# One crossbar transpose a chunk for q and k together, issued one or two loads behind the chunk's own load

## The chip, the cores and the metric

The kernel runs on one core of a Trainium2 chip. The metric is the device time of one execution in microseconds (us), median of several runs; the profile shows one execution, whose span is 1.7 to 1.9 us shorter than its time. Engines: PE is TensorE, POOL is GpSimd, DVE is VectorE, ACT is ScalarE, SP is the sequencer that issues nearly all DMAs here, in program order. The "rings" of the text are the queues that hold issued transfers for the DMA engines; a transfer "lands" when its data has arrived.

## The reference

Retention (8 batches, 8 heads, 576 tokens of 64), then a gated feed-forward block over 4608 tokens:

```python
scores = scale * np.matmul(q, k.transpose(0, 1, 3, 2))
Dmat = np.where(rel >= 0, gamma[:, None, None] ** rel[None, :, :], 0.0)
attn = np.matmul(scores * Dmat, v)                     # (B, H, S, D)
x = attn.transpose(0, 2, 1, 3).reshape(B * S, H * D)   # 4608 x 512
gate = 1.0 / (1.0 + np.exp(-(x @ w_gate)))             # d_ff = 1536
out = (gate * (x @ w_val)) @ w_out
```

## The kernel before

Tokens are cut into 40 chunks, five a batch: four of 128 tokens and one of 64. Chunks 0 to 3 go another way; chunks 4 to 39 are the subject. For each, three loads (v, k, q; 256 KB each) bring fp32 tiles; POOL scales and casts k into a block-diagonal tile, scales and casts q, and casts v; SP transposes k and q through the crossbar; PE makes scores (`qk`), updates a running state (`st`, copied to SBUF by DVE as `sbd`) and combines both (`pv`). The feed-forward matmuls of finished tokens fill PE between these phases.

```python
def cast_k(s):
    ...
    kn = kbd[s % 3]                      # block-diagonal, wiped once
    for j in range(n // 64):
        for hh in range(2):
            nc.gpsimd.tensor_tensor(out=kn[half(hh), j, :, half(hh)], in0=k32[half(j), hh::2, :], ...)

def cross(s):
    ...
    t = att_pool.tile([P, 2, M, P], BF16, tag="kT", bufs=3)     # 8 blocks of 128 columns
    nc.sync.dma_start_transpose(out=t[:, 0:nj]..., in_=natural["k", s][:, 0:nj]...)
    t = att_pool.tile([P, M, P], BF16, tag="qT", bufs=5)        # 4 blocks
    nc.sync.dma_start_transpose(out=t[:, :, 0:n], in_=natural["q", s][0:n]...)

def casts_to(s):
    while done["cast"] <= min(NS - 1, s):
        x = done["cast"]
        cast_k(x); cast_q(x); cross(x); cast_v(x)
        done["cast"] += 1

def run_phase(kind, s):
    if kind == "qk":
        loads_to(s + LEAD_LOAD)          # 5
        casts_to(s + LEAD_CAST)          # 2
        phase_qk(s)
        ...
```

So at the scores of chunk s, SP is given the loads up to s + 5 and then the transposes of s + 2: three chunks' loads stand ahead of a transpose.

Of the kernel before, what the change touches and what calls it, by code (L numbers as in the profile page):

```python
# [10 lines left out]
BF16 = mybir.dt.bfloat16  # L11
# [5 lines left out]
def kernel(  # L17
# [19 lines left out]
    nc = tc.nc  # L37

    B, H, S, D = q.shape
    NT, DM = out.shape  # L40
    DFF = moe_w_gate.shape[1]
    P = 128
    M = H // 2
# [4 lines left out]
    consts = ctx.enter_context(tc.tile_pool(name="consts", bufs=1))  # L48
    ld_pool = ctx.enter_context(tc.tile_pool(name="ld", bufs=18))
    nat_pool = ctx.enter_context(tc.tile_pool(name="nat", bufs=4))  # L50
    att_pool = ctx.enter_context(tc.tile_pool(name="att", bufs=3))
# [13 lines left out]
    STEPS = [(b, c) for b in range(B) for c in range(NC)]  # L65
    width = [min(P, S - c * P) for c in range(NC)]
# [8 lines left out]
    def load(s):  # L75
        b, c = STEPS[s]
        n = width[c]
        t0 = c * P
        tiles = []
        for nm, src in (("v", v), ("k", k), ("q", q)):  # L80
            t = ld_pool.tile([P, H, D], FP32, tag="ld", name=f"{nm}32_{s}")
            nc.sync.dma_start(out=t[0:n], in_=src[b, :, t0:t0 + n, :].rearrange("h p d -> p h d"))
            tiles.append(t)
        loaded[s] = tiles
# [21 lines left out]
    def load_wo(f):  # L106
        t = ld_pool.tile([P, DM], FP32, tag="ld", name=f"wo32_{f}")
        nc.sync.dma_start(out=t, in_=moe_w_out[f * P:(f + 1) * P, :])
        parts["o", f] = t
# [6 lines left out]
    load(4)  # L116
    load_w(8, 4)
    load(5)
    for f in range(3):
        load_wo(f)  # L120
    LEAD_LOAD = 5
    LEAD_CAST = 2


# [3 lines left out]
    def fill(n):  # L128

        ps = ffn_psum.tile([P, 512], FP32, tag="ffn", name=f"idle_{fill.at}")  # L130
        fill.at += 1
        for i in range(n):
            nc.tensor.matmul(ps, lhsT=blank[:, 0:P], rhs=blank, start=True, stop=True)
# [37 lines left out]
                                base=0, pattern=[[-1, 2], [1, P]], channel_multiplier=-2)  # L171
    NB = 4
    vbd = [consts.tile([P, 2, M, P], BF16, name=f"vbd{i}") for i in range(NB)]
    kbd = [consts.tile([P, 2, M, P], BF16, name=f"kbd{i}") for i in range(3)]
    tri = consts.tile([P, 64], BF16)

    def later_constants():

        nc.gpsimd.memset(tri, 1.0)
        for p0 in (0, 64):  # L180
            nc.gpsimd.affine_select(out=tri[p0:p0 + 64], in_=tri[p0:p0 + 64], compare_op=ALU.is_ge, fill=0.0,
                                    base=0, pattern=[[1, 64]], channel_multiplier=-1)
        for t in kbd:
            nc.gpsimd.memset(t, 0.0)


# [4 lines left out]
    def cast_w(nm, f, nf, i, eng):  # L191
        r = NKC // nf
        at = (slice(None), slice(i * r, (i + 1) * r), slice(f * P, (f + nf) * P))
        eng(out=(wg_sb if nm == "g" else wv_sb)[at], in_=parts.pop((nm, f, i)))  # L194
# [9 lines left out]
    natural = {}  # L204
    turned = {}
# [13 lines left out]
    def cast_k(s):  # L219

        b, c = STEPS[s]
        n = width[c]
        k32 = loaded[s][1]
        kn = kbd[s % 3]
        for j in range(n // 64):
            for hh in range(2):
                nc.gpsimd.tensor_tensor(  # L227
                    out=kn[half(hh), j, :, half(hh)], in0=k32[half(j), hh::2, :],
                    in1=ktab[half(j), c, hh::2].unsqueeze(2).to_broadcast([64, M, D]), op=ALU.mult)
        natural["k", s] = kn  # L230

    def cast_q(s):
        b, c = STEPS[s]
        n = width[c]
        q32 = loaded[s][2]
        qs = nat_pool.tile([P, H, D], BF16, tag="qs", name=f"qs_{s}")
        nc.gpsimd.tensor_tensor(out=qs[0:n], in0=q32[0:n],  # L237
                                in1=qtab[0:n, c, :].unsqueeze(2).to_broadcast([n, H, D]), op=ALU.mult)
        natural["q", s] = qs

    def cast_v(s):

        b, c = STEPS[s]
        n = width[c]
        v32 = loaded[s][0]
        vb = vbd[s % NB]
        for j in range(n // 64):
            for hh in range(2):
                nc.gpsimd.tensor_copy(out=vb[half(hh), j, :, half(hh)], in_=v32[half(j), hh::2, :])  # L249
        natural["vb", s] = vb  # L250

    def cast_dense(s, j):

        if s >= NS or STEPS[s][1] == NC - 1:
            return
        if j == 0:
            natural["vs", s] = nat_pool.tile([P, 2, M, D], BF16, tag="vs", name=f"vs_{s}", bufs=2)
        for hh in range(2):
            nc.scalar.copy(out=natural["vs", s][half(hh), j], in_=loaded[s][0][half(j), hh::2, :])  # L259

    def cross(s):

        n = width[STEPS[s][1]]
        nj = n // 64
        t = att_pool.tile([P, 2, M, P], BF16, tag="kT", name=f"kT_{s}", bufs=3)
        nc.sync.dma_start_transpose(out=t[:, 0:nj].rearrange("p j m t -> p (j m) t"),
                                    in_=natural["k", s][:, 0:nj].rearrange("p j m d -> p (j m d)"))
        turned["k", s] = t
        t = att_pool.tile([P, M, P], BF16, tag="qT", name=f"qT_{s}", bufs=5)
        nc.sync.dma_start_transpose(out=t[:, :, 0:n],  # L270
                                    in_=natural["q", s][0:n].rearrange("p h d -> p (h d)"))
        turned["q", s] = t

    turned = {}

# [5 lines left out]
    def half(x):  # L281
        return slice(x * 64, x * 64 + 64)
# [46 lines left out]
    def tile_sv(s, eng):  # L329
        sb = sbd[s % 4]  # L330
        for hh in range(2):
            eng(out=sb[half(hh), :, half(hh)], in_=st_tiles[STEPS[s][0]][half(hh)])
        state[s, 1] = sb
# [28 lines left out]
    def phase_qk(s):  # L362
        n = width[STEPS[s][1]]
        nj = n // 64
        kT, qT = turned["k", s], turned["q", s]
        pt = att_pool.tile([P, M, P], BF16, tag="pt", name=f"pt_{s}")
        qkp = qk_psum.tile([P, M, P], FP32, tag="qk", name=f"qk_{s}")
        for j in range(nj):
            for m in range(M):
                nc.tensor.matmul(qkp[:, m, half(j)], lhsT=kT[:, j, m, :], rhs=qT[:, m, half(j)],  # L370
                                 start=True, stop=True)
        nc.vector.tensor_tensor(out=pt[:, :, 0:n].rearrange("p m (j t) -> p m j t", t=64),  # L372
                                in0=qkp[:, :, 0:n].rearrange("p m (j t) -> p m j t", t=64),
                                in1=tri.unsqueeze(1).unsqueeze(1).to_broadcast([P, M, nj, 64]), op=ALU.mult)
        probs[s] = pt

    def phase_pv(s):
        b, c = STEPS[s]
        n = width[c]
        t0 = first_tok[s]  # L380
        qT = turned["q", s]
        pt = probs.pop(s)
        vb = natural["vb", s]
        pvp = pv_psum.tile([P, M, P], FP32, tag="pv", name=f"pv_{s}")
        for j in range(n // 64):
            before = state.get((s, j - 1) if j else (s - 1, 1)) if c or j else None
            for m in range(M):
                if before is not None:
                    nc.tensor.matmul(pvp[:, m, half(j)], lhsT=before[:, m, :], rhs=qT[:, m, half(j)],  # L389
                                     start=True, stop=False)  # L390
                nc.tensor.matmul(pvp[:, m, half(j)], lhsT=vb[:, j, m, :], rhs=pt[:, m, half(j)],  # L391
                                 start=before is None, stop=True)
        nc.scalar.copy(out=xT[:, :, t0:t0 + n], in_=pvp[:, :, 0:n])  # L393
# [27 lines left out]
    done = {"ld": PAIRED + 2, "cast": PAIRED}  # L421

    def loads_to(s):
        while done["ld"] <= min(NS - 1, s):
            load(done["ld"])
            done["ld"] += 1

    def casts_to(s):
        while done["cast"] <= min(NS - 1, s):
            x = done["cast"]  # L430
            cast_k(x)
            cast_q(x)
            cross(x)
            cast_v(x)
            done["cast"] += 1

    def run_phase(kind, s):
        if kind == "qk":
            loads_to(s + LEAD_LOAD)
            casts_to(s + LEAD_CAST)  # L440
            phase_qk(s)
            cast_dense(s, 1)
        elif kind == "pv":
            phase_pv(s)
            cast_dense(s + 1, 0)
        else:
            phase_st(s, int(kind[2]))
# [146 lines left out]
    cast_pair("k", 1, 0, nc.gpsimd)  # L594
    cast_pair("k", 1, 1, nc.gpsimd)
    tile_sv(1, on_act)
    fill(3)

    h_first((0,), 0, 2 * P)
# [34 lines left out]
    casts_to(4)  # L634
    for i in range(4):
        cast_w("g", 8, 4, i, on_pool)
    for f in range(3, 8):
        load_wo(f)
    casts_to(5)
    for f in range(8, NFC):  # L640
        load_wo(f)
    loads_to(6)
# [19 lines left out]
        cast_wo(f, on_pool)  # L662
    loads_to(7)
    casts_to(6)
    loads_to(8)
    h_first((10, 11), 0, 4 * P)
    at = 0

# [62 lines left out]
```

## Time and profile before

| | before |
|---|---|
| time, median of 3 | 359.12 us (359.04 to 359.7) |
| span of the profiled run | 357.5 us |
| PE idle, 57.7 to 103.7 us | 13.3 us |
| PE waits for a transposed q | 12.0 us, 6 times |
| POOL waits for PE's states (buffer of k) | 66.7 us, 30 times |
| transposes | 72 |

The page's first part gives busy times, its second 40 equal slices of the span. Lists by engine name a line of the kernel, what it writes and reads, and what ended the idle time before it. The lines that carry the reading stand in the prediction below.

### The profile page before, as it was taken

What the parts mean: (1) busy time and instruction counts of PE and PEld (TensorE: products, weight loads), DVE (VectorE), ACT (ScalarE), POOL (GpSimd) and SP (SyncE); (2) the same over time, 40 slices, a digit from 0 to 9 for tenths busy, and PEclk for the clock granted to TensorE, in tenths of its full rate; (3) what the DMA queues carried; (4) which work ended last, traced back from release to release, by engine and by line L of the source; (5) the groups of instructions that cost most, each with busy time, mean ns of one, the idle gap of its engine ahead of it and who ended that gap; (6) DMA issues with size and microseconds to landing.
All of it is one profiled execution on the core that took longest, in us unless ns stands there. A gap on an engine that the chain in (4) does not pass through costs nothing.

```text
span 357.5 us, 7682 instructions
## 1 busy us (share of the span) xinstructions
PE 334.3 (94%) x2868; PEld 191.7 (54%) x2868; DVE 162.9 (46%) x344; ACT 171.2 (48%) x356; POOL 187.5 (52%) x335
## 2 busy tenths in 40 slices
PE   7899985967699999999999899999999999999996
PEld 3565443855575655655655555554455545544443
DVE  4656520534374653742644653553356345512420
ACT  6765324424455645545545555544465455533321
POOL 7446657958682796367534894576437950000000
PEclk9999999889999999999999999999999999999999
DMA  8999999999999999996997999997599440011002
GB/s 227 314 329 286 251 265 173 208 217 215 181 178 210 212 138 211 212 181 139 166 163 164 161 172 242 211 156 155 148 175 204 115 113 14 0 61 59 2 25 93
DMA packets 169396, 60.27 MB, mean 169 GB/s; under 512 B 152848, under 2 KB 161296, under 8 KB 169360
## 3 DMA queue, kind: packets, MB, share of 16 engines
q1 hardware_dynamic: 169216, 59.66, 84.0%
q8 instruction: 22, 0.36, 0.4%
q14 instruction: 14, 0.11, 0.2%
q10 hardware_dynamic: 144, 0.13, 0.1%
HBM read 37.75 MB, written 9.44 MB: 132 GB/s over the span
## 4 chain that ended last, share of the span: by engine, by line
PE 73%; DMA 10%; POOL 9%; issue 3%; DVE 1%; ACT 1%; SPq 1%; POOLq 0%; DVEq 0%; ACTq 0%
PE h L464 43%; PE op L527 20%; POOL kbd L227 5%; DMA qT<-qs 3%; POOL vbd L249 2%; PE qk L370 2%; PE st L403 2%; POOL qs L237 2%; DMA kT<-kbd 2%; DMA k<-in_k_dram 2%; PE pv L391 2%; DMA q32p<-in_q_dram 1%; PE pv L389 1%; DMA v<-in_v_dram 1%; DMA wo<-in_moe_w_out_dram 1%
## 5 line engine op out<-in xcount | busy, mean ns | idle before, releaser
L227 POOL TENSOR_TENSOR kbd<-k,ktab 64x256 bf16<-64x256 f32 x128 | 78.5, 613 | 86.5 <-PE st L403 66.7
L464 PE MATMUL h<-xT,wv_sb 128*128 128x512 bf16 (+3 forms) x592 | 119.5, 325 | 0.2 <-ACT g L487 0.2
L464 PE MATMUL h<-xT,wg_sb 128*128 128x512 bf16 (+3 forms) x592 | 119.3, 325 | 0.0
L491 DVE TENSOR_TENSOR gv<-g,h 128x512 bf16<-128x512 bf16 (+1 forms) x104 | 65.2, 627 | 69.0 <-PE h L464 53.1
L487 ACT ACTIVATE g<-h 128x512 bf16<-128x512 f32 (+1 forms) x104 | 56.9, 548 | 70.8 <-PE h L464 60.9
L527 PE MATMUL op<-wo_sb,gv 128*128 128x512 bf16 x372 | 85.5, 379 | 0.0
L464 PEld LDWEIGHTS <-wg_sb 128*128 128x128 bf16 x592 | 53.0, 100 | 35.3 <-issue 0.3
L464 PEld LDWEIGHTS <-wv_sb 128*128 128x128 bf16 x592 | 53.1, 100 | 32.9 <-DVE wv_sb L194 0.6
L409 DVE CAST sbd<-st 64x256 bf16<-64x256 f32 x112 | 47.1, 421 | 16.3 <-PE st L403 13.9
L372 DVE TENSOR_TENSOR pt<-qk,tri 128x512 bf16<-128x512 f32 (+1 forms) x36 | 22.7, 630 | 68.8 <-PE qk L370 68.5
L527 PEld LDWEIGHTS <-gv 128*128 128x128 bf16 x372 | 34.4, 98 | 36.3
L249 POOL CAST vbd<-v 64x256 bf16<-64x256 f32 x128 | 50.8, 397 | 4.9
L259 ACT CAST vs<-v 64x256 bf16<-64x256 f32 x112 | 45.1, 403 | 1.8
L499 ACT COPY ob<-op 128x512 f32<-128x512 f32 x35 | 20.3, 587 | 53.1 <-PE op L527 42.9
L237 POOL TENSOR_TENSOR qs<-q,qtab 128x512 bf16<-128x512 f32 (+1 forms) x36 | 37.6, 1044 | 2.8
L393 ACT CAST xT<-pv 128x512 bf16<-128x512 f32 (+1 forms) x36 | 19.4, 538 | 27.5 <-PE pv L391 27.4
L370 PE MATMUL qk<-qT,kT 128*128 128x64 bf16 x256 | 13.7, 196 | 12.0 <-DMA qT<-qs 12.0
L370 PEld LDWEIGHTS <-kT 128*128 128x128 bf16 x256 | 12.7, 99 | 18.5 <-DMA kT<-kbd 10.8
L477 ACT ACTIVATE g<-h 128x256 bf16<-128x256 f32 x32 | 12.2, 384 | 20.2 <-PE h L464 18.4
L403 PEld LDWEIGHTS <-kbd 128*128 128x128 bf16 x224 | 13.6, 98 | 15.3 <-POOL kbd L227 3.3
L403 PE MATMUL st<-vs,kbd 128*128 128x64 bf16 x224 | 15.8, 193 | 3.6 <-DVE sbd L409 3.0
L391 PE MATMUL pv<-pt,vbd 128*128 128x64 bf16 x256 | 19.2, 193 | 0.0
(66 smaller groups left out, 178.8 us busy)
## 6 DMA issues: line engine op xcount, KB each, us to landing
out_dram<-ob SPq DMA_DIRECT2D x35, 256.0 KB, 2.3
v<-in_v_dram SPq DMA_DIRECT2D x28, 256.0 KB, 3.9
k<-in_k_dram SPq DMA_DIRECT2D x28, 256.0 KB, 4.4
q<-in_q_dram SPq DMA_DIRECT2D x28, 256.0 KB, 5.0
wg<-in_moe_w_gate_dram SPq DMA_DIRECT2D x12, 256.0 KB, 5.7
wv<-in_moe_w_val_dram SPq DMA_DIRECT2D x12, 256.0 KB, 5.6
wo<-in_moe_w_out_dram SPq DMA_DIRECT2D x12, 256.0 KB, 3.9
k32p<-in_k_dram SPq DMA_DIRECT2D x4, 256.0 KB, 4.7
```

The lines of the kernel that those rows point to most:

```text
L227: nc.gpsimd.tensor_tensor(out=kn[half(hh), j, :, half(hh)], in0=k32[half(j), hh::2, :], in1=ktab[half(j), c, hh::2].unsqueeze(2).to_broadc ...
L237: nc.gpsimd.tensor_tensor(out=qs[0:n], in0=q32[0:n], in1=qtab[0:n, c, :].unsqueeze(2).to_broadcast([n, H, D]), op=ALU.mult)
L249: nc.gpsimd.tensor_copy(out=vb[half(hh), j, :, half(hh)], in_=v32[half(j), hh::2, :])
L259: nc.scalar.copy(out=natural["vs", s][half(hh), j], in_=loaded[s][0][half(j), hh::2, :])
L370: nc.tensor.matmul(qkp[:, m, half(j)], lhsT=kT[:, j, m, :], rhs=qT[:, m, half(j)], start=True, stop=True)
L391: nc.tensor.matmul(pvp[:, m, half(j)], lhsT=vb[:, j, m, :], rhs=pt[:, m, half(j)], start=before is None, stop=True)
L403: nc.tensor.matmul(st_tiles[b][:, m, :], lhsT=natural["k", s][:, j, m, :], rhs=natural["vs", s][:, j, m, :], start=(c == 0 and j == 0 and ...
L409: nc.vector.tensor_copy(out=sb[half(hh), :, half(hh)], in_=st_tiles[b][half(hh)])
L464: nc.tensor.matmul(out, lhsT=w_sb[:, kc, fc * P:(fc + 1) * P], rhs=xT[:, kc, t0 + a:t0 + e], start=(kc == 0), stop=(kc == NKC - 1))
L487: nc.scalar.activation(out=g[:, 0:n], in_=h1[:, 0:n], func=AF.Sigmoid)
L491: nc.vector.tensor_tensor(out=gvs[some[0]][:, a:e], in0=g[:, 0:n], in1=h2[:, 0:n], op=ALU.mult)
L527: nc.tensor.matmul(opp, lhsT=gvs[fc][:, nb * P:(nb + 1) * P], rhs=wo_sb[:, fc, :], start=(fc == 0), stop=(fc == NFC - 1))
```

## The change

Its intent: halve the transposes by laying q and the two diagonal k blocks side by side in one tile, and bring each transpose out from behind the loads of later chunks. The natural tile has four buffers, not three; two are wiped by DVE early on. The core of the diff:

```diff
-    for f in range(3):
+    for f in range(2):
         load_wo(f)
-    kbd = [consts.tile([P, 2, M, P], BF16, name=f"kbd{i}") for i in range(3)]
+    qk_nat = [consts.tile([P, 3, M, P], BF16, name=f"qk_nat{i}") for i in range(NB)]   # NB = 4
@@ cast_k, cast_q
-        kn = kbd[s % 3]
+        kn = qk_nat[s % NB][:, 1:3]
-        qs = nat_pool.tile([P, H, D], BF16, tag="qs", name=f"qs_{s}")
+        qs = qk_nat[s % NB][:, 0].rearrange("p m (hh d) -> p (m hh) d", d=D)
@@ cross: the two transposes give way to
+        nb = 1 + width[STEPS[s][1]] // 64
+        t = att_pool.tile([P, 3, M, P], BF16, tag="T", name=f"T_{s}", bufs=4)
+        nc.sync.dma_start_transpose(out=t[:, 0:nb].rearrange("p j m t -> p (j m) t"),
+                                    in_=qk_nat[s % NB][:, 0:nb].rearrange("p j m d -> p (j m d)"))
@@ casts_to, run_phase
             x = done["cast"]
+            loads_to(x + (1 if x < 10 else 2))
             cast_k(x)
...
-            loads_to(s + LEAD_LOAD)
             casts_to(s + LEAD_CAST)
```

In the start-up part chunk 5's casts are written out, so that they pull no loads forward, and the early load of chunk 8 goes.

## The prediction

> **What bounds the kernel now.** I read the page first, for busy time and its 40 slices. TensorE (PE) is the bound almost everywhere:
>
> ```profile
> PE 334.3 (94%) x2868; PEld 191.7 (54%) x2868; DVE 162.9 (46%) x344; ACT 171.2 (48%) x356; POOL 187.5 (52%) x335
> ...
> PE   7899985967699999999999899999999999999996
> ...
> PEclk9999999889999999999999999999999999999999
> ```
>
> The span is 357.5 us and PE is busy 334.3, so 23.2 us is all that can be won by feeding PE sooner, plus what two dips of its clock cost. The slices that are not full stand at both ends and from the seventh to the twelfth, about 54 to 107 us. Busy time by stretch puts a number on it:
>
> ```profile
> 0.00:45.00 45.00, 41.59 (x411) 23.07 (x412) 25.46 (x63) 25.91 (x52) 26.16 (x50) 1.00 1.04 281
> 45.00:57.70 12.70, 11.40 (x90) 5.68 (x88) 2.81 (x6) 5.12 (x12) 7.34 (x13) 1.00 1.18 252
> 57.70:103.70 46.00, 32.67 (x435) 27.82 (x435) 18.48 (x54) 18.49 (x46) 34.63 (x62) 0.93 1.05 190
> 103.70:190.00 86.30, 86.12 (x734) 51.23 (x733) 42.72 (x87) 44.80 (x97) 50.06 (x90) 1.00 1.03 182
> 190.00:220.00 30.00, 28.24 (x270) 16.65 (x268) 15.97 (x33) 16.78 (x37) 23.09 (x41) 1.00 1.23 179
> ```
>
> First is the stretch and its length, then PE's busy time. Between 57.7 and 103.7 us PE idles 46.00 - 32.67 = 13.3 us; between 190 and 220, 1.8 us; from 103.7 to 190 only 0.2. So the question is what PE waits for in the third row. The table of waits:
>
> ```profile
> PE qk L370 <- DMA qT<-qs: 12.0, 6, 4.2
> ...
> PE st L403 <- DVE sbd L409: 3.0, 5, 1.0
> ```
>
> 12.0 us in six waits is the arrival of a transposed q: chunk 6 at 61.96 us (4.23 us of waiting), chunk 7 at 75.17 (2.34), chunk 8 at 83.03 (1.43), chunk 9 at 91.24 (0.37), chunk 10 at 97.14 (2.77): 11.1 us in this stretch. The sixth, 0.9 us, falls after 200 us. Why it is late stands in the timeline of the DMA-issuing queue (start, length, issue):
>
> ```profile
> 57.42 1.87 SPq L266 DMA_TRANSPOSE kT<-kbd  x1
> 59.38 1.21 SPq L270 DMA_TRANSPOSE qT<-qs  x1
> ...
> 65.26 0.57 SPq L82 DMA_DIRECT2D v<-in_v_dram  x1
> 65.87 1.11 SPq L82 DMA_DIRECT2D k<-in_k_dram  x1
> 67.03 1.46 SPq L82 DMA_DIRECT2D q<-in_q_dram  x1
> 68.59 3.86 SPq L266 DMA_TRANSPOSE kT<-kbd  x1
> 72.55 1.20 SPq L270 DMA_TRANSPOSE qT<-qs  x1
> ```
>
> Chunk 7's casts end on GpSimd (POOL) at 64.05 us, but its transposes stand behind the loads of chunks 8, 9 and 10: k goes out at 68.59, that issue takes 3.86 us because the rings are full, q follows at 72.55 and lands 2.6 us later. Thus **PE waits for an order in a queue**, not for DMA or POOL capacity; both are busy but neither is full (POOL works 34.63 of 46 us).
>
> **The Trainium skill.** (1) "DMA: Bandwidth & Descriptors", section Queues, rings and completion order: descriptors are consumed in ring order on each DMA engine. The 3.86 us issue behind nine loads agrees. (2) The same page, section Rules for kernel authors: coalesce many small transfers. The trace agrees only in part: with nothing else moving (274 to 293 us) a four-block transpose issues in 1.20 us and an eight-block one in 1.23 to 1.31, so issue time is nearly free of size; but the landing grows from 2.4 to about 3.4 us for 512 more packets of 256 B. (3) "TensorE: Matmul & The Clock Gate", section The HAM clock gate: after an idle window of about 3.4 us the clock halves. The trace agrees: 0.51 granted from 61.4 to 64.8 us, 0.50 from 75.1 to 78.5, just after the two longest idle stretches of this part. No page tells what twelve blocks cost; my figure is worked out from the trace.
>
> **The change, part by part.**
>
> *One transpose for two.* A full chunk is now one transfer of twelve blocks, not eight and four; the bytes stay (a half-width chunk moves eight blocks, not six). Issue: 36 issues of about 1.2 us go. Latency in a quiet queue: before, k issue 1.3 plus q's 2.6 to land is about 4.0 us; after, 3.4 plus 1.0 for 512 more packets is an estimated 4.4 us. So merging alone gains nothing for one chunk, and q's early half no longer starts before q is cast (k used to go out one cast, 1.04 us, earlier). Its gain is the issue time where the queue is the limit: from 37 to 52 us SP issues without pause, and chunks 4 and 5 save 1.24 and 1.47 us there, so the load of chunk 6 goes out about 2.5 us sooner than the 49.1 us of before.
>
> *Transposes ahead of loads.* For chunk x only the load of x+1 (x under 10) or x+2 stands ahead, where three more chunks stood. A chunk's load is 3072 packets of 256 B; the trace moves about 855 of them in a microsecond, 3.6 us a chunk. A transpose takes about 2.4 us of the engines.
>
> *Four buffers, not three,* for the natural k: POOL waited 66.7 us in 30 times for PE to finish the states of three chunks back. It may now run a chunk (some 5.6 us of POOL) further ahead.
>
> *Wipes.* POOL wipes two tiles of 1536 columns for three of 1024, the same work. Two more wipes go to DVE near 14 us; 512 columns of the same kind took 0.48 us, so 768 take an estimated 0.72 each, 1.44 in all, in a gap of 1.63 us (13.87 to 15.50). Nothing on the path.
>
> *The new schedule worked out* (my arithmetic, from the durations above and 5.54 us of POOL a chunk, the distance from chunk 7's first cast at 60.29 us to chunk 8's at 65.83):
> - k of chunk 6 lands near 52.4 us (54.7 before), its casts end near 56.3, the transpose lands near 60, after load 7 leaves the engines. PE needs it at 56.8. Start of chunk 6 on PE: 60, against 61.96: **2 us won.** If the load does not come sooner, it lands at 62.8 and 0.9 us is lost here.
> - Chunk 7 lands near 66, chunk 8 near 72, chunk 9 near 79. PE's own work puts its needs at 60 + 10.6 = 70.6, then 75.5, then 83.3: no wait. I took PE's distances between chunks from the trace and left out the DMA waits; the second clock dip (3.4 us at half, about 1.5 us lost) goes with the wait before it.
> - Chunk 10 waits for two loads ahead of it (11 and 12, where the lead changes from one to two, and a store that follows PE): an estimated 88.7, needed at 86.7. A **new wait of 2 us.** Chunk 11 lands about 95.5, needed at 95.0.
> - So chunk 11 starts on PE near 95.5, where the trace has 103.3 to 103.5: **8 us won.** Chunk 12 was needed only at 112.06, so from there PE is full again.
> - 190 to 215 us: POOL runs chunk after chunk at about 6 us and PE idles 1.8 us for it. One more chunk of lead covers this: **1.3 us**, less than the whole as the DMA share is at its highest there.
>
> Sum: 8 + 1.3 = 9.3 us, 359.1 - 9.3 = 349.8, taken as **350 us**. The stages before 45 us and after 220 are the same work and PE is full in both.
>
> **The rivals.**
>
> *POOL or the load takes over the wait.* With one load of lead, POOL may finish a chunk and find the next k not landed: 3.6 us of load behind 2.4 of transpose and up to three stores (256 KB at some 340 GB/s, 0.75 us each) is over 7 us against POOL's 5.5. For: the queue is in order, so every wait for POOL also holds back the next load. Against: I have counted most of this and slack of 3 to 4 us is left at chunks 7 to 9. If it bites at each chunk by 1 us more, half the gain goes: about 354 to 355 us.
>
> *The merged transfer is slow.* Between two transposes in a row the engines moved only 97 to 99 GB/s (59 to 60, 72 to 74 us) though they count as busy; twelve blocks could be as slow all through. Then chunk 6 starts later than before and the whole string shifts by 2 to 3 us: about 353. The opposite, that the gap between the two transfers is what is slow and goes, would give 347.
>
> *The waits were hidden anyway.* The wait of PE for DVE's states (3.0 us) and the DMA rate stay. Against: the six waits fall on PE, the bound, and the idle time of the stretch matches them. If only the order mattered for chunk 7 and others fell back on POOL, 355 to 356.
>
> *A loss* would need transposes in the full stretch after 104 us to come late with the shorter lead. PE uses a chunk each 8.9 us there ((316 - 103) / 24), POOL and DMA need an estimated 5.5 to 6.9, so I give it little.
>
> **Range and chances.** The middle is 350. If the load of chunk 6 comes no sooner I get about 352.5 to 353, with that and the first rival 355; with both clock dips gone and no new wait at chunk 10, 346.5. Faster by over 2% means below 351.9, and my middle is only 2 us under it: 0.64. Within 2%: 0.34. Slower: 0.02.
>
> **What the changed profile should show.** PE busy in about 57 to 96 us of 80% or more, not 71%. The total of PE's waits for transposes down from 12.0 to 4 to 6 us, the longest still at chunk 6 (about 3 us), one at chunk 10. The SP timeline with one transpose of 1.3 to 2 us issue a chunk, landing in 4 to 5.5 us. The clock dip at 75 us gone. POOL's waits for PE's states well below 66.7 us before 110 us, with some waits for k loads in their place. Idle time near 190 to 215 below 1 us. I am wrong if chunk 6 starts later than 62 us, if POOL's waits for k loads grow past 5 us between 60 and 100, or if PE shows new gaps after 110 us.

## The result, and the profile after

The changed kernel took **353.8 us** (352.06 to 354.28, 4 runs) beside 359.41 us (359.04 to 359.9, 4 runs). The ratio is 0.9839, 95% interval 0.9806 to 0.9872. Ratios here are the mean time of one kernel's fast runs over the mean of the other's fast runs of the same rounds, so not quite the ratio of the medians. The time lies in the predicted range, 3.8 us above the predicted middle, and the change falls within 2%, the outcome to which the prediction gave a chance of 0.34. The profiled run was the fastest (352.06 us), so I ran the kernel again (below: 353.26 us); where the two profiles differ I say so.

The page after, same parts as the prediction's first fence:

```profile
PE 332.4 (95%) x2868; PEld 190.5 (54%) x2868; DVE 163.7 (47%) x346; ACT 171.2 (49%) x356; POOL 187.7 (54%) x334
...
PE   7899994987999999999999999999999999999996
...
PEclk9999998799999999999999999999999999999999
```

PE's work is the same 2868 matmuls; the weak slices now end four slices sooner. Busy time by stretch (stretch and its length, then PE's busy time; the last three numbers are the granted clock, the DMA share and GB/s):

```profile
57.70:103.70 46.00, 38.83 (x493) 31.40 (x494) 22.08 (x62) 21.19 (x51) 36.97 (x67) 0.93 1.10 212
59.50:66.30 6.80, 5.41 (x57) 5.41 (x58) 2.42 (x7) 1.04 (x3) 6.21 (x11) 0.50 1.13 230
75.10:78.50 3.40, 3.10 (x70) 3.08 (x71) 1.44 (x6) 1.80 (x5) 0.45 (x1) 1.00 1.32 237
190.00:220.00 30.00, 28.93 (x258) 16.06 (x257) 16.61 (x34) 15.79 (x34) 23.25 (x42) 1.00 1.24 210
```

The idle time between 57.7 and 103.7 us fell from 13.3 to 7.2 us, that between 190 and 220 from 1.8 to 1.1. The half-rate clock at 75 us is gone, but 6.8 us of it now stand in one piece after the wait at chunk 6, as much as the two dips of before together; the repeat has 3.4 us (0.51 from 62.4 to 65.8). What PE still waits for:

```profile
PE qk L365 <- DMA T<-qk_nat: 5.1, 2, 4.5
PE st L398 <- DVE sbd L404: 4.6, 7, 1.9
```

12.0 us of waits for transposes became 5.1, nearly all at chunk 6; PE's waits for DVE's states grew from 3.0 to 4.6 us (in the repeat 2.4 us are put down to DVE and 2.2 to POOL). That PE now comes to them sooner is my reading. The queue of DMA issues, against the 68.59 and 72.55 us of before for chunk 7:

```profile
62.60 1.42 SPq L264 DMA_TRANSPOSE T<-qk_nat  x1
64.12 1.94 SPq L501 DMA_DIRECT2D out_dram<-ob  x3
66.11 0.66 SPq L82 DMA_DIRECT2D v<-in_v_dram  x1
66.82 0.70 SPq L82 DMA_DIRECT2D k<-in_k_dram  x1
67.56 0.63 SPq L82 DMA_DIRECT2D q<-in_q_dram  x1
68.31 2.94 SPq L264 DMA_TRANSPOSE T<-qk_nat  x1
```

Chunk 7's transpose goes out at 62.60 us, when its casts end, and chunk 8's follows in 5.7 us with three stores and one load (the 64 tokens of chunk 9) between. On POOL the wait changed its name, first the kernel before, then the changed one:

```profile
POOL kbd L227 <- PE st L403: 66.7, 30, 7.5
POOL kbd L227 <- DMA k<-in_k_dram: 9.9, 3, 5.5
```

```profile
POOL qk_nat L227 <- DMA k<-in_k_dram: 31.3, 11, 9.5
...
POOL qk_nat L227 <- PE st L398: 7.6, 6, 1.8
```

With the shorter lead POOL waits for loads, not for buffers. Between 60 and 100 us that is 4.8 us of it, in two waits; later it costs little, as PE idles 0.3 us from 103.7 to 190.

### The profile page after: what moved, and what is told of

It is laid out like the page before. It is cut to its first block, busy times and chain, and to the rows that moved or that the text cites. A ratio compares the mean times of both kernels' runs of the same rounds, so it can differ in the third digit from the quotient of the medians.

```text
span 350.2 us, 7624 instructions
## 1 busy us (share of the span) xinstructions
PE 332.4 (95%) x2868; PEld 190.5 (54%) x2868; DVE 163.7 (47%) x346; ACT 171.2 (49%) x356; POOL 187.7 (54%) x334
## 4 chain that ended last, share of the span: by engine, by line
PE 75%; DMA 9%; POOL 5%; DVE 3%; issue 3%; SPq 3%; ACT 2%; POOLq 0%; DVEq 0%; ACTq 0%
PE h L459 42%; PE op L522 22%; DMA k<-in_k_dram 5%; DMA T<-qk_nat 3%; POOL qk_nat L227 3%; PE qk L365 2%; PE st L398 2%; PE pv L386 2%; PE pv L384 2%; DMA q32p<-in_q_dram 1%; DVE sbd L404 1%; POOL qk_nat L237 1%; POOL vbd L248 1%; SPq L82 1%; PE op L512 1%
## 5 line engine op out<-in xcount | busy, mean ns | idle before, releaser
L227 POOL TENSOR_TENSOR qk_nat<-k,ktab 64x256 bf16<-64x256 f32 x128 | 78.4, 613 | 69.2 <-DMA k<-in_k_dram 31.3
L459 PEld LDWEIGHTS <-wg_sb 128*128 128x128 bf16 x592 | 53.0, 100 | 35.4 <-issue 0.3
L404 DVE CAST sbd<-st 64x256 bf16<-64x256 f32 x112 | 47.0, 420 | 15.7 <-PE st L398 13.3
L367 DVE TENSOR_TENSOR pt<-qk,tri 128x512 bf16<-128x512 f32 (+1 forms) x36 | 22.7, 630 | 62.8 <-PE qk L365 62.5
L237 POOL TENSOR_TENSOR qk_nat<-q,qtab 128x512 bf16<-128x512 f32 (+1 forms) x36 | 37.5, 1042 | 3.1 <-DMA q<-in_q_dram 0.4
L398 PEld LDWEIGHTS <-qk_nat 128*128 128x128 bf16 x224 | 13.6, 98 | 16.3 <-POOL qk_nat L227 3.5
L398 PE MATMUL st<-vs,qk_nat 128*128 128x64 bf16 x224 | 15.8, 194 | 4.8 <-DVE sbd L404 4.6
L365 PEld LDWEIGHTS <-T 128*128 128x128 bf16 x256 | 12.2, 99 | 11.4 <-DMA T<-qk_nat 5.9
L365 PE MATMUL qk<-T 128*128 128x64 bf16 x256 | 13.6, 195 | 5.1 <-DMA T<-qk_nat 5.1
```

The costliest lines, as they stand in the source:

```text
L237: nc.gpsimd.tensor_tensor(out=qs[0:n], in0=q32[0:n], in1=qtab[0:n, c, :].unsqueeze(2).to_broadcast([n, H, D]), op=ALU.mult)
L365: nc.tensor.matmul(qkp[:, m, half(j)], lhsT=kT[:, j, m, :], rhs=qT[:, m, half(j)], start=True, stop=True)
L398: nc.tensor.matmul(st_tiles[b][:, m, :], lhsT=natural["k", s][:, j, m, :], rhs=natural["vs", s][:, j, m, :], start=(c == 0 and j == 0 and ...
L404: nc.vector.tensor_copy(out=sb[half(hh), :, half(hh)], in_=st_tiles[b][half(hh)])
L459: nc.tensor.matmul(out, lhsT=w_sb[:, kc, fc * P:(fc + 1) * P], rhs=xT[:, kc, t0 + a:t0 + e], start=(kc == 0), stop=(kc == NKC - 1))
```

## The experiments

Twelve runs, each timed in five rounds beside the kernel before. First the starts of chunks' scores on PE in the profiles, in us, with PE's distance from chunk 6 to 11 (the stretch the prediction worked out). A profile is one run: that of "order, four buffers" was 1.6 us quicker than its median, the others lie within 0.8 us of theirs, but for the first one of the change.

| kernel | time, median | ratio (95%) | chunk 6 | chunk 10 | chunk 11 | 6 to 11 |
|---|---|---|---|---|---|---|
| before | 359.1 to 359.6 | 1 | 61.96 | 97.14 | 103.30 | 41.3 |
| changed, first profile | 353.8 | 0.9839 (0.9806 to 0.9872) | 60.90 | 89.5 | 96.51 | 35.6 |
| changed, repeat | 353.26 | 0.9817 (0.9793 to 0.984) | 62.33 | 90.2 | 97.69 | 35.4 |
| merge only | 356.08 | 0.9898 (0.9875 to 0.9921) | 61.94 | 94.75 | 100.9 | 39.0 |
| order only | 356.09 | 0.9901 (0.9878 to 0.9924) | 62.87 | 93.49 | 101.07 | 38.2 |
| order, four buffers | 356.89 | 0.9915 (0.9887 to 0.9944) | 61.83 | 91.90 | 99.40 | 37.6 |
| merge and order, three buffers | 352.77 | 0.9805 (0.9769 to 0.9842) | 62.12 | 90.3 | 97.27 | 35.2 |

### The changed kernel again

No edit.

> The changed kernel once more, unaltered: a second look at a typical execution, since the profiled one (352.06 us) was the fastest of five. All theories: 353.5 to 354.3 us, 1.4 to 1.7% below before, with the gain standing at 6 to 7 us at chunk 11 of the profile.

353.26 us, 0.2 us under the range I gave; the gain at chunk 11 is 5.6 us, under the 6 to 7 I gave. The interval reaches across 2%, so whether the change is worth 2% stays unclear. The first profile had a start-up 0.9 us quicker: chunk 5 already stood at 48.7 us against 49.5 here and 49.4 before. It won another 0.5 us on the way to chunk 6; from there to chunk 11 the two agree to 0.3 us.

### Merge alone, order alone

Theory: the gain is the order, as predicted. Rival: it is the halved number of transposes. Merge alone keeps the loads as far ahead as before and three natural buffers (the core, against the changed kernel):

```diff
+            loads_to(s + LEAD_LOAD)            # back, LEAD_LOAD = 5
-            loads_to(x + (1 if x < 10 else 2))
-    qk_nat = [... for i in range(NB)]
+    qk_nat = [... for i in range(3)]
```

> One transpose a chunk, but loads four ahead as before and three natural buffers. Theory 'order' (transposes stood behind three chunks of loads): at most 1 to 1.5 us of the 5.6 come back, 357.9 to 358.9 us, and chunk 7 still starts on PE after 74 us. Theory 'merge' (36 fewer issues and no stall between two transposes are the gain): 354 to 355 us.

356.08 us: 3.6 us won, between the two expectations, and more than the 1.5 us the prediction's theory allowed. Chunk 7 gains only 0.2 us, but then each chunk a little more (0.9 at chunk 8, 1.3 at 9, 2.4 at 10). Why, in the queue. First the kernel before around chunk 8, then merge alone:

```profile
78.12 2.09 SPq L266 DMA_TRANSPOSE kT<-kbd  x1
80.31 1.21 SPq L270 DMA_TRANSPOSE qT<-qs  x1
81.61 1.01 SPq L506 DMA_DIRECT2D out_dram<-ob  x2
...
85.21 3.38 SPq L266 DMA_TRANSPOSE kT<-kbd  x1
```

```profile
77.36 2.93 SPq L265 DMA_TRANSPOSE T<-qk_nat  x1
80.39 1.00 SPq L502 DMA_DIRECT2D out_dram<-ob  x2
...
84.06 3.56 SPq L265 DMA_TRANSPOSE T<-qk_nat  x1
```

The chunk's own latency is nearly the same, 4.9 us from k's issue to q's landing (82.98) against 4.8 (82.12). What is shorter is the time until SP is free again: 3.4 us before, 2.9 merged. SP issues without a pause here, each chunk's loads and transposes behind the last one's, so this adds up over the chunks: from chunk 7's transpose to chunk 11's is 29.8 us before (68.6 to 98.4) and 27.0 merged (68.4 to 95.4). An issue is not SP's own work alone: the 17 transposes whose issue takes about 2 us or more between 57 and 104 us (before, merge alone, the repeat) all end it 0.5 to 1.7 us before the last load ahead of them lands. I read this as rings that are full: no view shows the rings.

Order alone takes the load calls of the change and keeps `kbd`, two transposes and three buffers:

> Two transposes and three natural buffers as before, only the order of loads and transposes is that of the change. Theory 'order': 354.5 to 355.5 us, chunk 10 starts on PE near 91 us (97.1 before, 89.5 changed). Theory 'merge': 358 us or more. Theory 'buffer' (the fourth natural buffer lets the casts run ahead): 357 to 358 us.

356.09 us, 3.6 us won: the "order" theory's 354.5 to 355.5 is missed. The transposes no longer stand behind three chunks, and chunk 8 starts 3.7 us sooner; but of the waits for a transposed q

```profile
PE qk L369 <- DMA qT<-qs: 7.6, 4, 4.3
```

1.8 us at chunk 10 and 1.3 at chunk 11 remain beside the 4.3 at chunk 6. The two halves nearly add up: 3.6 and 3.6 against 5.6 to 6.4 for both. Neither theory alone holds.

### The fourth buffer

Order with four `kbd` buffers, and the change with three:

```diff
-    kbd = [... for i in range(3)]
+    kbd = [... for i in range(4)]
```

> Two transposes, four natural buffers, the order of the change. Theory 'order': the same as with three buffers up to 190 us and 0.3 to 1 us less after, 354 to 355 us. Theory 'buffer': 354 us against 357 to 358 with three. Theory 'merge': 358 us or more.

> The change with three natural buffers in place of four. Theory 'the fourth buffer carries nothing' (order and merge alone gave 3.6 us each and the change 6.4): 352.8 to 353.8 us. Theory 'buffer': 355 us or more, with PE idle again near 200 us.

356.89 us with four against 356.09 with three; 352.77 with three against 353.26 with four. The differences lie inside the intervals and neither favours the fourth buffer: it carries nothing that these runs can see, and the 354 to 355 us given for two transposes are missed with it as without it. Near 200 us (190 to 220), where the prediction gave it 1.3 us, PE idles 1.1 to 1.2 us in the changed kernel's two profiles and 1.1 with three buffers. Merge alone and order alone leave 1.4 us there, of 1.8 before. Single profiles can't part so small a gain further.

### How many transposes

The clearest test of the merge: the changed kernel with the same bytes in two or three issues.

```diff
-        nc.sync.dma_start_transpose(out=t[:, 0:nb]..., in_=qk_nat[s % NB][:, 0:nb]...)
+        for lo, hi in ((1, nb), (0, 1)):        # two issues; three: one for each j
+            nc.sync.dma_start_transpose(out=t[:, lo:hi]..., in_=qk_nat[s % NB][:, lo:hi]...)
```

> The change, its transpose cut into two issues (k blocks, then the q block) that both wait for all casts; bytes, order and buffers unchanged. Theory 'the number of issues costs': 356 to 357 us, as the run with order and four buffers but two transposes (356.9). Theory 'what counts is something else of the merge, such as the place of the q tile or of the buffers': 353 to 354 us.

> The same cut into three issues of four blocks each. Theory 'the number of issues costs': another 2 to 4 us over two issues, 358 to 361 us. Theory 'something else': 353 to 354.5 us.

One issue 353.26, two 357.62 (ratio 0.9943, 0.9899 to 0.9986), three **365.96 us** (1.0174, 1.014 to 1.0209), beyond what I expected. So the number of transposes costs, with their bytes unchanged. The queue with three, and the busy time of 57.7 to 103.7 and 103.7 to 190 us:

```profile
66.59 4.17 SPq L265 DMA_TRANSPOSE T<-qk_nat  x3
70.86 1.50 SPq L501 DMA_DIRECT2D out_dram<-ob  x3
```

```profile
57.70:103.70 46.00, 32.99 (x406) 26.27 (x405) 16.70 (x49) 17.54 (x43) 32.59 (x59) 0.85 0.95 183
103.70:190.00 86.30, 83.58 (x736) 51.10 (x735) 44.04 (x91) 44.68 (x97) 54.15 (x97) 1.00 0.95 172
```

Three transposes of 128 KB take 4.17 us to issue, three stores of 256 KB 1.50. Each of these transposes lands 0.5 to 0.8 us after the one before it, or 1.0 to 1.4 where the next was issued late, but takes 1.27 us to issue; so SP cannot keep the engines fed with small ones. The engines show it: they move 183 GB/s here, against 212 in the changed kernel. A store's issue (0.38 to 0.53 us) is shorter than its landing distance (0.6 to 1.3 us in the kernel before and with merge alone), so it can hide behind its own data. That the issue time is the cause is my reading of these lines; that the count costs is shown. Not all of the loss with three is queue time: the granted clock is 0.50 for 17.0 us of this profile (51.9 to 55.3, 62.1 to 68.9, 96.3 to 103.1 us), against 0.51 for 3.4 us in the repeat. PE is busy for 12.5 and 3.4 us of these; if half of that is lost, an estimated 4.5 us of the 12.7 are the clock's.

### Stores off the queue

If SP's time is what is short, taking the stores away should help the kernel before:

```diff
-                nc.sync.dma_start(out[x[1]:x[1] + P, :], x[2])
+                nc.scalar.dma_start(out[x[1]:x[1] + P, :], x[2])
```

> The kernel before with its 32-odd output stores issued by ScalarE's queue instead of the one queue that issues loads and transposes; all bytes and their order among loads and transposes unchanged. Theory 'the issuing queue itself is what is full between 57 and 103 us' (40 of 43 us issuing): six stores of 0.5 us leave it there, 2 to 3 us won, 356.4 to 357.4 us. Theory 'the DMA engines are full': no gain, 359 to 359.6 us.

> Loads k, q, v and the stores issued by ScalarE's queue. In the changed kernel only 1.0 us of waits for transposes is left after chunk 6, so the queue has little more to give: 350.5 to 351.5 us, 0 to 1 us under k, q, v alone. If ScalarE's issues of half a microsecond come back as late sigmoids: 352 us or more.

358.36 us (0.9969, 0.9943 to 0.9994), and 354.86 us for the second (0.9863, 0.9835 to 0.9892), worse than k, q, v alone (351.5 us, below). The first lies between the two theories' figures. My expectation was wrong in saying that the order stays. From another queue the stores overtake:

```profile
56.03 0.38 ACTq L506 DMA_DIRECT2D out_dram<-ob  x1
...
58.39 0.34 ACTq L506 DMA_DIRECT2D out_dram<-ob  x1
```

```profile
64.48 0.59 PE L370 MATMUL qk<-qT,kT 128*128 128x64 bf16 x8 [5.46 <-DMA qT<-qs]
```

The first stores went out at 73.85 us before and go at 56 and 58 now, ahead of the transposes of chunk 6 (58.71 us); its wait grows from 4.23 to 5.46 us and chunk 7 starts 3.6 us later. From there to chunk 10 the kernel is 3.6 us quicker (18.4 against 22.0 us), but the stores' bytes have also left that stretch. So this run cannot tell issue time from engine time, and stays inconclusive. In the second run, too, chunk 6 waits longer (5.5 us, against 3.8 with k, q, v alone) and starts 2.1 us later; a wait for late sigmoids is not among PE's largest. What the runs do show is that another queue changes who goes first.

### A lead of two for all chunks

```diff
-            loads_to(x + (1 if x < 10 else 2))
+            loads_to(x + 2)
```

> The change with two loads ahead of every chunk's transpose, also of chunks 6 to 9 which had one. Theory 'each load ahead costs its 3.6 us of the rings only where PE is waiting': chunks 7 to 9 land near 72, 78 and 82 us, just at PE's need, chunk 10's cast starts 3 to 4 us sooner; 352.8 to 354.3 us, the same. Theory 'fewer loads ahead is what wins': 355 us, half way to the four-ahead kernel with one transpose (356.1).

355.6 us (0.9896, 0.9872 to 0.992), which looks like the second theory. The profile says otherwise: the same line pulled the load of chunk 6 ahead of the output weights (its k went out at 38.4 us, not 48.8), and PE waited for those:

```profile
47.47 1.46 PE L672 MATMUL op<-wo_sb,gv 128*128 128x512 bf16 x6 [2.06 <-POOL wo_sb L199]
```

Chunk 5 starts at 52.85 us, 3.3 late, and from chunk 6 to 11 PE takes 34.6 us, no longer than with a lead of one (35.4). In these two profiles a lead of two is as good as one in that stretch, and the early edge spoiled the total; a run with only the stretch changed was not made.

### The wait at chunk 6

The largest wait left runs from the landing of k over its casts to the transpose. Loading k, q, v in that order brings k first:

```diff
-        for nm, src in (("v", v), ("k", k), ("q", q)):
+        for nm, src in (("k", k), ("q", q), ("v", v)):
```

> The change with a chunk's loads issued k, q, v in place of v, k, q. Theory 'the wait at chunk 6 runs from the landing of k over its casts to the transpose': k lands 1.2 us sooner and chunk 6 starts on PE 0.8 to 1.2 us sooner, 352 to 352.6 us. Theory 'the transpose waits for the DMA engines to finish the load of chunk 7 anyway': within 0.3 us of the change, 353.3 us.

> Loads k, q, v, and eight units of the first 128-token FFN block (3.6 us of PE) placed ahead of chunk 6's scores, where PE waits 4.5 us for the transpose. If that wait is pure idle time that other ready work can fill, 1.5 to 3.5 us under the run with k, q, v alone (351.5): 348 to 350 us. If the chunks after it are bound by queue and casts, the time comes back as waits at chunks 7 to 11: 351 to 352 us.

351.5 us (0.9783, 0.9743 to 0.9824): chunk 6 starts at 61.04 us after a wait of 3.76. It is the lowest median of all, 1.8 us under the repeat of the change, but the two intervals overlap, so I call it likely and not settled. The second run also puts eight units of feed-forward work (3.6 us of PE) ahead of chunk 6's scores. PE's timeline:

```profile
60.08 0.41 PE L365 MATMUL qk<-T 128*128 128x64 bf16 x8 [0.59 <-DMA T<-qk_nat]
66.62 0.41 PE L365 MATMUL qk<-T 128*128 128x64 bf16 x8 [0.86 <-DMA T<-qk_nat]
...
87.82 0.41 PE L365 MATMUL qk<-T 128*128 128x64 bf16 x8 [3.16 <-DMA T<-qk_nat]
```

The wait at chunk 6 is filled and chunk 7 starts 5.2 us sooner than with k, q, v alone, the clock dip included; but chunk 10 then waits 3.16 us, and from chunk 11 on only 0.8 us is left. The time is 352.54 us (0.9798, 0.977 to 0.9826): nothing won. This profile was the run's quickest (350.44 us), and those 0.8 us equal its lead from the start-up (chunk 5 at 48.7 us, 49.5 with k, q, v alone). Between chunks 6 and 11 it takes 34.9 us, as k, q, v alone does (34.7): PE's idle time was only moved about. That loads, casts and transposes set the pace there is the reading that fits.

## Why the prediction was right or wrong

- **What bounds the kernel: right.** PE's waits for transposes were the place, and they fell from 12.0 to 5.1 us (5.6 in the repeat), within the 4 to 6 foretold. The stretch from chunk 6 to chunk 11 was foretold to shrink from 41.3 to 35.5 us (60 to 95.5) and measured 35.4 and 35.6. This one term carries the result, but that it was met so closely is partly luck. From chunk 8 to 9 PE took 8.8 us in both profiles, where 7.8 was foretold (it waited 1.9 us for a state of chunk 8); from 9 to 10 it took 3.4 where 5.4 was foretold, as the "new wait of 2 us" at chunk 10 did not come; from 10 to 11, 7.0 and 7.5 for 6.8, with a wait of 0.6 to 1.0 us at chunk 11. The errors cancel.
- **"Thus PE waits for an order in a queue": half of it.** Order alone brings 3.6 us, merge alone 3.6. Its "not for DMA ... capacity" stays open, as the long issues end only when the loads ahead of them have nearly landed.
- **"So merging alone gains nothing for one chunk ... Its gain is the issue time where the queue is the limit: from 37 to 52 us": the step that failed as mechanism.** The latency part was right (4.9 us against 4.8), though its estimate of 4.4 us for twelve blocks was high (3.8 at chunk 6 in both profiles) and so were the "2.4 us of the engines": with merge alone six transposes landed 1.0 to 1.3 us after the load before them. But I looked for the full queue only before 52 us, while the lines I had printed myself show SP issuing back to back from 65 to 74 us. There the second issue is paid once a chunk, 0.7 us from chunk 7 to 11 ((29.8 - 27.0) / 4). The schedule used merged transposes throughout, so the sum held what the argument denied.
- **"Start of chunk 6 on PE: 60 ... 2 us won": the step that failed by the most.** The measure is 62.33 us in the repeat, 0.4 later than before (past the 62 us that I had named as a sign of being wrong), and 60.90 in the quick run. In the repeat the issue time saved at chunk 4 did not reach the load of chunk 6; the queue reads:

```profile
42.89 1.91 SPq L264 DMA_TRANSPOSE T<-qk_nat  x1
44.89 3.36 SPq L108 DMA_DIRECT2D wo<-in_moe_w_out_dram  x4
...
48.82 0.53 SPq L82 DMA_DIRECT2D k<-in_k_dram  x1
```

  Chunk 5's transpose had to wait for its q cast, which ended at 42.7 us, and the four weight loads behind it took 3.36 us to issue against 1.95 before. k went out at 48.82, 0.3 us sooner, not 2.5. My fallback (62.8 and 0.9 us lost) was the nearer figure. In the quick run k did go out 2.6 us sooner (46.56), yet its cast could begin only 1.5 us sooner than the 54.74 of before:

```profile
53.28 2.65 POOL L227 TENSOR_TENSOR qk_nat<-k,ktab 64x256 bf16<-64x256 f32 x4 [1.81 <-DMA k<-in_k_dram]
```

  So a load that goes out sooner need not land as much sooner: here it stood behind weight loads and a transpose that landed one after another up to 50.80 us.
- **"190 to 215 us ... 1.3 us": mis-sized,** 0.5 us from chunk 11 to the end in both profiles, and 0.6 with three buffers; the cause named, the fourth buffer, was wrong.
- **What was left out:** PE's waits for states were taken as fixed and grew by about 1.6 us. The second clock dip went as foretold, but in the first profile the first one doubled. "PE is full in both" of the outer stages was misread: before 45 us it is busy 41.59 us of 45. So was "just after the two longest idle stretches": the 2.77 us before chunk 10 are longer than the 2.34 before chunk 7, and no dip follows them.
- **The sum.** Foretold 2 + 5.8 + 1.3 = 9.1 us by these terms. The repeat's profile has -0.4 + 6.0 + 0.5 = 6.1, its span 357.5 - 351.4 = 6.1. The 3 us between are chunk 6 and the 190 us term. The chance of 0.64 for a gain above 2% leaned on both, and that gain did not come.

## What to carry to other kernels

Where a queue issues without pause, price an operation by the time until the queue is free for the next, not by its own latency: it is paid once a turn. Count crossbar transposes, not only their bytes, and put q and k into one if the casts allow it. Before claiming that a saved issue starts a later load sooner, look for the next item in the queue that waits for something else; and before claiming that it lands sooner, look at what is still in flight ahead of it.

## What the Trainium skill lacked or had wrong

- "DMA: Bandwidth & Descriptors", section DMA Transpose (X-bar): it gives no issue time for a transpose within SBUF; the page's only sequencer figures for transposes stand in its passage on trn3 and are for other sizes. Here it is 1.20 us for four blocks and 1.27 to 1.5 for twelve where little else was in flight, against 0.4 to 0.6 us for a plain 256 KB transfer; cutting the transposes into three (two for half-width chunks), 64 issues more, cost 12.7 us.
- "Advanced Engine Details and Errata", section X-Bar Transpose (TRN2), calls them as fast as regular DMAs. For the data alone this fits: in the merge-alone run six transposes (five of 384 KB, one of 256 KB) landed 1.0 to 1.3 us after the load before them, a load of 256 KB 1.1 to 1.2 us. For the whole it does not, as the issue is two to four times a plain one's.
- "DMA: Bandwidth & Descriptors", section Rules for kernel authors, on spreading DMAs over queues: it says that this only saves the sequencer's issue time. Here it also changed the order: stores moved to ScalarE went out 12 to 18 us sooner, and chunk 6's q transpose landed at 64.4 us against 61.9 (1.3 us of it the run was late already at chunk 5).
- "TensorE: Matmul & The Clock Gate", section The HAM clock gate, asks for an idle window of about 3.4 us. In the kernel before, the clock halved at 75.1 us after a window in which PE had been busy 1.12 of 3.4 us: a window need not be wholly idle.
